# Token sums taken in place from 15 shared block buffers, weight splits in batches: attention followed by a fast maxout product

## The chip, the core and the metric

The kernel runs on one core of one Trainium2 chip. The metric is the device time in microseconds of one execution. The engines are TensorE (PE; its weight loads are PEld), VectorE (DVE), ScalarE (ACT), GpSimd (POOL) and SyncE (SP), which issues almost all DMAs from one queue, in order.

## What is computed

Sigmoid attention for 8 batches of 12 heads (448 tokens, head size 64), and then a product network on the 3584 tokens of 768 features, all in float32:

```python
scores = scale * np.matmul(q, k.transpose(0, 1, 3, 2)) - np.log(S)
attn = 1.0 / (1.0 + np.exp(-scores))
out = np.matmul(attn, v)                   # then heads are put side by side: x
h = np.maximum(np.maximum(x @ w1, x @ w2), x @ w3)
return h @ w_out
```

## The kernel before

**Attention** runs over 24 units: 8 batches, and 3 groups of four heads in each. A unit makes its scores on PE, the sigmoid on ACT, and the weighted sums on PE. Each float32 operand is split into a high and a low part (`hi`, `lo`) so that PE's products keep their precision; DVE splits the queries and keys of the next unit while PE works on this one (`qk_split`, lines 362 and 363). `finish` (lines 435 to 437) brings a half unit's result out of PSUM, by an ACT copy and a DVE addition, into a tile `m0` or `m1`, of which there is one each, and SP stores it to DRAM. The next copy into the same tile waits for that store.

**The network** has three stages (w1 and w2 with w3 go through stages 0 and 1, w_out through stage 2) of four visits, one for each pair of batches: 12 visits. A visit makes a 768 by 768 block product by 15 products of sums instead of 18 plain ones (`PRODUCTS`, one step each). A step has 18 matmuls in stages 0 and 1 and 12 in stage 2. Its operands are 15 sums of weight blocks (`W_SUMS`) and blocks `b0` to `b5` of the tokens or sums of them (`X_SUMS`, 11 of these).

- **Token sums** (`token_sums`, lines 256 to 276) are made on POOL, for each pair twice, because a half holds 448 columns: SP loads a half of the six blocks into the one tile `xin`, POOL makes 11 sums into six tiles `s`, SP stores each to `t_dram`. Layer 0 (the attention's output) has its first three pairs done during attention and the fourth at the start of stage 0. Layer 1 (h) has its four pairs done from stage 1's second visit on.
- **Loads of a step** (`x_load`) bring a block or a sum, 128x896, from DRAM into one of four tiles `qk`, five steps ahead. `x_split` makes `hi` on ACT (line 321) and `lo` (line 322) on DVE or, in the five steps where DVE has results to combine, on POOL, two steps ahead.
- **Weights** come packed and are decoded in pieces (`decode`: two ACT and four DVE instructions); three pieces make a group, for which POOL makes 15 sums of 128x128 (line 206). For stage 0 DVE splits the 15 operands one by one (`w_split`, lines 236 and 237), five at the head of a unit. Later stages' operands go through DRAM and are split by `w_resplit`.

What runs where is set by the order of the calls: each engine takes its instructions in that order. `work` hands POOL its sums, weight sums first; `later` and `tick` delay stores. `take` and `give` do not exist yet.

Of the kernel before, what the change touches and what calls it, by code (L numbers as in the profile page):

```python
# [45 lines left out]
X_SUMS = (  # L46
    ("s7", "b3", "b1"),
    ("s0", "s7", "b2"),
    ("s2", "b3", "b2"),
    ("s3", "b5", "b3"),  # L50
    ("s6", "b4", "b0"),
    ("s15", "s6", "s7"),
    ("s8", "b5", "s6"),
    ("s11", "s8", "b1"),
    ("s5", "b4", "b2"),
    ("s9", "b2", "b5"),
    ("s16", "b4", "b5"),
# [22 lines left out]
def attention_then_maxout(  # L80
# [30 lines left out]
        [dram.tile([P, NK, 2 * S], F32, name=f"x_dram{layer}{p}") for p in range(PAIRS)]  # L111
        for layer in range(2)
    ]
    t_dram = [
        [dram.tile([P, len(X_SUMS), 2, S], F32, name=f"t_dram{layer}{p}") for p in range(PAIRS)]
        for layer in range(2)
    ]
# [15 lines left out]
    qk_p = pool(ctx, "qk", 4)  # L133
    xin_p = pool(ctx, "xin", 1)
    s_p = pool(ctx, "s", 6)
# [7 lines left out]
    w_ops = [None] * len(PRODUCTS)  # L143
# [51 lines left out]
    def weight_sums(st, q, kk, wd):  # L195
# [3 lines left out]
        def one(n, name, a, op, b):  # L199
            if n == 0:  # L200
                while w_splits:
                    w_split()
                blocks["all"] = sums_p.tile([P, (len(SUMMED) + len(temps)) * P], F32, name="sums")
# [5 lines left out]
            if n == len(W_SUMS) - 1:  # L209
                if st == 0:  # L210
                    w_splits.extend((i, q, kk, blocks[w]) for i, (w, *_) in enumerate(PRODUCTS))
                else:
                    later.append((now[0], store))
# [13 lines left out]
    def w_tiles(i):  # L227
        w_ops[i] = [w_p.tile([P, 3 * 2 * P], F32R, name=f"w{part}_{i}") for part in ("hi", "lo")]

    def w_split():  # L230
        i, q, kk, src = w_splits.pop(0)
        if w_ops[i] is None:
            w_tiles(i)
        cols = slice((2 * q + kk) * P, (2 * q + kk + 1) * P)
        hi, lo = (t[:, cols] for t in w_ops[i])
        pin(nc.vector.tensor_copy(out=hi, in_=src))
        pin(nc.vector.tensor_tensor(out=lo, in0=src, in1=hi.bitcast(F32), op=sub))  # L237

    def w_load(st, i):
        w_tiles(i)  # L240
        n = UNITS[st]
        dst = w_ops[i][1].bitcast(F32)[:, : n * 2 * P]
        pin(nc.sync.dma_start(
            out=dst.rearrange("p (q k c) -> p q k c", k=2, c=P),
            in_=w_dram[st][:, :, :, SLOT[PRODUCTS[i][0]]],
        ))

    def w_resplit(st, i, engine):
        cols = slice(0, UNITS[st] * 2 * P)
        hi, lo = (t[:, cols] for t in w_ops[i])  # L250
# [5 lines left out]
    def token_sums(layer, p, when):  # L256
        index = {name: k for k, (name, *_) in enumerate(X_SUMS)}
        src = x_dram[layer][p][:].rearrange("p (j two) t -> p two j t", two=2)

        def one(kk, name, a, b, r):  # L260
            if name == X_SUMS[0][0]:
                xin = xin_p.tile([P, 2 * M * S], F32, name="xin")
                pin(nc.sync.dma_start(
                    out=xin[:].rearrange("p (j t) -> p j t", j=M), in_=src[:, kk]
                ))
                r.update((f"b{k}", xin[:, k * S : (k + 1) * S]) for k in range(2 * M))
            s = r[name] = s_p.tile([P, S], F32, name="s")
            pin(nc.gpsimd.tensor_tensor(out=s, in0=r[a], in1=r[b], op=sub))  # L268
            later.append((now[0], lambda: pin(nc.sync.dma_start(
                out=t_dram[layer][p][:, index[name], kk], in_=s  # L270
            ))))

        for kk in range(2):
            r = {}
            for name, a, b in X_SUMS:
                x_work.append((1.3, when, lambda *to: one(*to), (kk, name, a, b, r)))

    def work(budget, most):
        while budget > 0:
            if w_work:  # L280
                cost, run = w_work.pop(0)
                run()
            elif x_work and most and now[0] >= x_work[0][1]:
                cost, _, run, to = x_work.pop(0)
                run(*to)
                most -= 1
            else:
                break
            budget -= cost
# [9 lines left out]
    x_raw, x_ops, xo_p = {}, {}, [hl_p]  # L299

    def x_load(g):
        if g >= total:
            return
        (st, p), name = visits[g // STEPS], PRODUCTS[g % STEPS][1]
        layer = st // LAST
        if name[0] == "b":
            j, th = divmod(int(name[1:]), 2)
            src = x_dram[layer][p][:, 2 * j : 2 * j + 2, th * S : (th + 1) * S]
        else:
            src = t_dram[layer][p][:, [s[0] for s in X_SUMS].index(name)]  # L310
        x_raw[g] = qk_p.tile([P, 2 * S], F32, name="qk")
        pin(nc.sync.dma_start(out=x_raw[g][:].rearrange("p (k s) -> p k s", k=2), in_=src))

    def x_split(g, copy, engine=nc.vector):
        if g >= total:
            return
        raw = x_raw.pop(g)
# [3 lines left out]
        pin(copy(out=hi, in_=raw))  # L321
        pin(engine.tensor_tensor(out=lo, in0=raw, in1=hi.bitcast(F32), op=sub))  # L322
        x_ops[g] = hi, lo

    def attention(stack):
# [3 lines left out]
        m_p = pool(stack, "m", 1)  # L331
# [3 lines left out]
        def load_qk(b, k):  # L335
            t = qk_p.tile([P, 2 * S], F32, name="qk")
            if b == k == 0:
                for cols in (slice(0, S + P), slice(S + P, 2 * S)):
                    pin(nc.sync.dma_start(out=t[:, cols], in_=qk[b, k, :, cols]))
            else:  # L340
                pin(nc.sync.dma_start(out=t, in_=qk[b, k]))
# [82 lines left out]
        def load(n):  # L424
# [3 lines left out]
            elif n < len(fours) + 2:  # L428
                for g in range(2):
                    x_load(2 * (n - len(fours)) + g)  # L430

        def finish(n, g, banks):
            b, f = fours[n]
            o = m_p.tile([P, S], F32, name=f"m{g}")
            pin(nc.scalar.copy(out=o, in_=banks[0][:, :S]))
            pin(nc.vector.tensor_tensor(out=o, in0=banks[1][:, :S], in1=o, op=add))  # L436
            pin(nc.sync.dma_start(
                out=x_dram[0][b // 2][:, 2 * f + g, b % 2 * S : (b % 2 + 1) * S], in_=o
            ))
# [13 lines left out]
        terms = [[(loads[0][0],) * 2]]  # L453
        end = len(fours) - 1
        for p in range(PAIRS - 1):
            token_sums(0, p, 2 * M * (p + 1) + 2)
        for n in range(len(fours)):
            ts = loads.pop(n)
            if n != 1:
                fetch()  # L460
            if n:
                if n < end:
                    vts[n + 1] = load_v(*fours[n + 1])
                for _ in range(5):
                    if w_splits:
                        w_split()
# [10 lines left out]
            if n == 0:  # L477
                held = accumulators()
                last_scores(ts, held)
                load(n + 2)  # L480
                vts[n + 1] = load_v(*fours[n + 1])
            ahead = loads.get(n + 1)
# [13 lines left out]
            if 0 < n < end:  # L496
                decode()
            tick(1)
            work(9.0, 5)
# [10 lines left out]
            if n < end:  # L510
                lasts[n + 1] = last_scores(ahead)
                load(n + 3)
            weigh(g1, vt, 1, chunks[1], True, range(1, C))
            finish(n, 1, g1)
        while w_splits:
            w_split()
# [5 lines left out]

    xo_p.append(pool(ctx, "xo", 2, reuse_waits="tile"))
    o_p = pool(ctx, "o", 3, reuse_waits="tile")
    ps_y = pool(ctx, "ps_y", 1, space=PSUM, reuse_waits="tile")

    x_load(4)
    token_sums(0, PAIRS - 1, now[0] + 1)
    layer_start = now[0]
    for p in range(PAIRS):  # L530
        token_sums(1, p, layer_start + (PAIRS + 1 + p) * STEPS + 2)
# [4 lines left out]
    def product(n, s, q):  # L536
# [6 lines left out]
        (w_hi, w_lo), (x_hi, x_lo) = w_ops[s], x_ops[n * STEPS + s]  # L543
        terms = [(w, x, k) for k in range(2) for w, x in ((w_lo, x_hi), (w_hi, x_lo), (w_hi, x_hi))]
        for m, (w, x, k) in enumerate(terms):
            pin(nc.tensor.matmul(  # L546
                ps[:, :S], w[:, (2 * q + k) * P : (2 * q + k + 1) * P], x[:, k * S : (k + 1) * S],
# [4 lines left out]
    def evacuate(n, s, q, y):  # L552
# [36 lines left out]
        elif q == UNITS[st] - 1:  # L589
            to, o = x_dram[1][p][:, M * st + i, th * S : (th + 1) * S], first[dst]  # L590
# [10 lines left out]

# [66 lines left out]
```

## Time and profile before

| | us |
|---|---|
| median of 2 runs (1005.02 to 1011.15) | 1008.09 |
| the profiled execution, whole | 1010.78 |
| its span | 1009.0 |
| attention, up to the first matmul of the network | 337.8 |
| network, first to last matmul | 664.8 |
| after the last matmul, in the span | 6.4 |
| PE busy, share of the span | 865.7 (86%) |
| DVE, ACT, POOL busy | 723.2, 494.7, 551.5 |

The busy time of DVE and POOL holds time in which an instruction had been issued and did not yet run. `PEclk` in the rows is the clock that was granted to PE, as a share of 2.4 GHz; 0.5 is its lower level.

### The profile page before, as it was taken

How to read it: one execution, taken by the hardware profiler on the slowest of the kernel's cores; microseconds unless marked ns; L12 is line 12 of the kernel's file. 1: busy time of each engine (PE TensorE's matmuls, PEld its weight loads, DVE VectorE, ACT ScalarE, POOL GpSimd, SP SyncE). 2: the span in 40 equal slices, each digit the busy share in tenths (PEclk: the TensorE clock that was granted, in tenths of full speed). 3: DMA queues.
4: the chain of work that ended last, by engine and by line, in shares of the span. 5: the costliest groups of instructions: out<-in, count | busy, mean ns of one | idle time of the engine just before them, and what ended most of it. 6: DMA issues, size and time to landing. Idle time of an engine off the chain costs nothing.

```text
span 1009.0 us, 15279 instructions
## 1 busy us (share of the span) xinstructions
PE 865.7 (86%) x5302; PEld 701.2 (69%) x5302; DVE 723.2 (72%) x1041; ACT 494.7 (49%) x698; POOL 551.5 (55%) x499
## 2 busy tenths in 40 slices
PE   9998958767684989998999989999999782958997
PEld 5554435434352678887999979888999672847986
DVE  5588575958583786899976988898886682544654
ACT  6886646546563543544445553434434451434462
POOL 0215345244615497578614754494956966759313
PEclk9999978797887898999999989999999897988999
DMA  7666477547763987877757764868798886989884
GB/s 251 228 212 236 136 296 261 201 167 272 266 216 130 354 304 217 291 240 255 262 184 252 245 215 159 281 207 283 256 285 285 284 287 219 348 283 329 304 267 164
DMA packets 127468, 250.57 MB, mean 248 GB/s; under 512 B 11168, under 2 KB 87712, under 8 KB 127392
## 3 DMA queue, kind: packets, MB, share of 16 engines
q1 hardware_dynamic: 127248, 249.49, 73.3%
q8 instruction: 42, 0.69, 0.3%
q14 instruction: 34, 0.28, 0.1%
q10 hardware_dynamic: 144, 0.11, 0.0%
HBM read 166.33 MB, written 83.23 MB: 247 GB/s over the span
## 4 chain that ended last, share of the span: by engine, by line
PE 47%; POOL 15%; DMA 15%; DVE 13%; issue 6%; ACT 2%; SPq 1%; DVEq 0%; POOLq 0%; ACTq 0%
PE y L546 37%; POOL s L268 8%; DMA t_dram<-s 6%; POOL sums L206 5%; PE ps_s L381 4%; DVE lo L322 2%; PE ps_s L405 2%; POOL lo L322 2%; DMA qk<-t_dram 2%; PE ps_av L405 2%; DMA xin<-x_dram 2%; DMA x_dram<-m 2%; DVE wd L186 1%; DVE wd L182 1%; DVE wlo L237 1%
## 5 line engine op out<-in xcount | busy, mean ns | idle before, releaser
L546 PE MATMUL y<-lo,whi 128*128 128x448 f32 x960 | 353.6, 368 | 46.7 <-POOL lo L322 45.7
L546 PE MATMUL y<-hi,wlo 128*128 128x448 f32 x960 | 354.0, 369 | 22.3 <-DVE c L576 12.8
L546 PE MATMUL y<-hi,whi 128*128 128x448 f32 x960 | 352.9, 368 | 0.0
L321 ACT CAST hi<-qk 128x896 fp32r<-128x896 f32 x178 | 164.9, 946 | 159.0 <-PE y L546 78.7
L268 POOL TENSOR_TENSOR s<-xin 128x448 f32<-128x448 f32 x112 | 152.0, 1377 | 142.5 <-DMA xin<-x_dram 70.2
L546 PEld LDWEIGHTS y<-lo,whi 128*128 128x128 f32 x960 | 183.7, 191 | 63.4 <-POOL lo L322 48.2
L546 PEld LDWEIGHTS y<-hi,wlo 128*128 128x128 f32 x960 | 183.5, 191 | 40.7 <-issue 20.7
L322 DVE TENSOR_TENSOR lo<-qk,hi 128x896 fp32r<-128x896 f32 x121 | 159.9, 1322 | 54.7 <-ACT hi L321 54.7
L546 PEld LDWEIGHTS y<-hi,whi 128*128 128x128 f32 x960 | 183.8, 191 | 12.5
L322 POOL TENSOR_TENSOR lo<-qk,hi 128x896 fp32r<-128x896 f32 x59 | 131.5, 2254 | 77.4 <-ACT hi L321 76.8
L351 ACT ACTIVATE a<-ps_s,bias_s 128x896 f32<-128x896 f32 x121 | 116.5, 1016 | 47.8 <-PE ps_s L381 46.5
L206 POOL TENSOR_TENSOR sums<-wd,wd 128x128 f32<-128x128 f32 x128 | 80.6, 649 | 59.0 <-DVE wd L187 38.0
L381 PE MATMUL ps_s<-hi 64*128 64x448 f32 x240 | 55.1, 455 | 64.3 <-DVE m L436 47.7
L381 PEld LDWEIGHTS ps_s<-hi 64*128 64x128 f32 x240 | 26.6, 217 | 88.3 <-DVE m L436 52.1
L570 ACT COPY d<-y 128x448 f32<-128x448 f32 x64 | 34.1, 535 | 80.4 <-PE y L546 76.9
L268 POOL TENSOR_TENSOR s<-s,xin 128x448 f32<-128x448 f32 x32 | 46.4, 1451 | 32.4 <-DMA t_dram<-s 30.6
L405 PE MATMUL ps_av<-a,v 64*64 64x448 f32 x576 | 62.6, 536 | 0.0
L576 DVE TENSOR_TENSOR c<-c,y 128x448 f32<-128x448 f32 x32 | 19.2, 614 | 56.6 <-PE y L546 56.6
L405 PE MATMUL ps_s<-a,v 64*64 64x448 f32 x576 | 59.7, 545 | 0.0
L363 DVE TENSOR_TENSOR lo<-qk,hi 128x896 fp32r<-128x896 f32 (+4 forms) x51 | 57.8, 1134 | 1.8
L186 DVE CUSTOM_DVE_ANT_0 wd<-wraw,wd 128x768 uint16<-128x768 uint16 x48 | 32.2, 670 | 29.4 <-ACT wraw L177 24.9
L252 POOL TENSOR_TENSOR wlo<-wlo,whi 128x768 fp32r<-128x768 f32 (+1 forms) x20 | 38.0, 1912 | 27.7 <-ACT whi L251 27.7
(73 smaller groups left out, 1144.4 us busy)
## 6 DMA issues: line engine op xcount, KB each, us to landing
qk<-t_dram SPq DMA_DIRECT2D x132, 448.0 KB, 4.8
t_dram<-s SPq DMA_DIRECT2D x176, 224.0 KB, 6.1
xin<-x_dram SPq DMA_DIRECT2D x16, 1344.0 KB, 8.4
qk<-x_dram SPq DMA_DIRECT2D x48, 448.0 KB, 4.7
qk<-qk SPq DMA_DIRECT2D x47, 448.0 KB, 4.7
wraw<-w SPq DMA_DIRECT2D x36, 384.0 KB, 5.8
v<-v SPq DMA_DIRECT2D x24, 448.0 KB, 6.3
x_dram<-m SPq DMA_DIRECT2D x48, 224.0 KB, 4.6
```

Of the source, the lines that this page charges most:

```text
L186: pin(nc.vector.tensor_tensor(out=bits, in0=bits, in1=low, op=ALU.add))
L206: pin(nc.gpsimd.tensor_tensor(out=blocks[name], in0=blocks[a], in1=blocks[b], op=add if op == "+" else sub))
L252: pin(engine.tensor_tensor(out=lo, in0=lo.bitcast(F32), in1=hi.bitcast(F32), op=sub))
L268: pin(nc.gpsimd.tensor_tensor(out=s, in0=r[a], in1=r[b], op=sub))
L321: pin(copy(out=hi, in_=raw))
L322: pin(engine.tensor_tensor(out=lo, in0=raw, in1=hi.bitcast(F32), op=sub))
L351: pin(nc.scalar.activation(out=a, in_=banks[:, :, :S], func=AF.Sigmoid, bias=bias_s, scale=scale))
L363: pin(nc.vector.tensor_tensor(out=lo[:, cols], in0=t[:, cols], in1=high.bitcast(F32), op=ALU.subtract))
L381: pin(nc.tensor.matmul(bank[e][:, :S], kt[r, S + c * P : S + (c + 1) * P], qt[r, :S], start=n == 0, stop=n == len(terms) - 1,))
L405: pin(nc.tensor.matmul(ps[e * D : (e + 1) * D, :S], vt[rows, (g * C + c) * 2 + e], chunks[c][rows, e], start=c == 0 and not (ahead and r = ...
L546: pin(nc.tensor.matmul(ps[:, :S], w[:, (2 * q + k) * P : (2 * q + k + 1) * P], x[:, k * S : (k + 1) * S], start=new and m == 0, stop=m == ...
L570: pin(nc.scalar.copy(out=mine[dst], in_=y))
```

## The change

**Buffers.** The tiles `qk` (4), `xin`, `s` (6) and `m0`, `m1` go. In their place are 15 tiles `raw` of 128x896 that everybody takes and gives back (`take`, `give`). If none is free, `take` issues delayed stores early until one is.

**Attention's results** stay in the tile in which `finish` writes them: the two halves of a unit are the two halves of one block. The sums of a pair are made from these tiles, whole (128x896), as soon as the blocks are there (`COME`): two after the unit whose number modulo 6 is 2, four after 4, five after 5. All four pairs are done so; the last nine sums of the last pair fall into the last unit and stage 0. Sums and blocks are still stored and reloaded for stages 0 and 1.

**Layer 1** is loaded (six blocks a visit), summed by POOL (`H_SUMS`) and split from the same tiles: no store to `t_dram`, no reload. Sums of visit n are made from six steps ahead of it to its fourth step.

**Order.** `work` gives POOL token sums first. `w_split` makes its 15 pairs in four batches, two batches a unit, at least one unit after the sums. Steps are split three ahead (`SPLIT`), loaded up to eight ahead (`AHEAD`), and in stage 2 every `lo` is on DVE.

```diff
+    slots = list(range(15))
+
+    def take():
+        while not slots:
+            later.pop(0)[1]()
+        k = slots.pop(0)
+        t = raw_p.tile([P, 2 * S], F32, name=f"raw{k}")
+        return t, k
+
+    def give(raw):
+        slots.append(raw[1])
...
-    def w_split():
-        i, q, kk, src = w_splits.pop(0)
+    def w_split(lag):
+        if not w_splits or w_splits[0][0] + lag > now[0]:
+            return
+        _, part, q, kk, sums, wd = w_splits.pop(0)
...
+        rows, src = (
+            (slice(0, 6), sums[:, 0:6]),
+            (slice(n, n + 2), threes[0][:, 0::2]),
+            (slice(6, n), sums[:, 6:n]),
+            (slice(n + 2, n + 4), threes[1][:, 0:2]),
+        )[part]
...
-            s = r[name] = s_p.tile([P, S], F32, name="s")
-            pin(nc.gpsimd.tensor_tensor(out=s, in0=r[a], in1=r[b], op=sub))
...
+    def x_sum(r, name):
+        _, a, b = X_SUMS[INDEX[name]]
+        r[name] = take()
+        pin(nc.gpsimd.tensor_tensor(out=r[name][0], in0=r[a][0], in1=r[b][0], op=sub))
...
+        def store():
+            pin(nc.sync.dma_start(out=t_dram[p][:, INDEX[name]], in_=r[name][0]))
+            if not keep:
+                give(r.pop(name))
...
         def finish(n, g, banks):
             b, f = fours[n]
-            o = m_p.tile([P, S], F32, name=f"m{g}")
+            p, k = b // 2, 2 * f + b % 2
+            if g == 0:
+                blocks[p][f"b{k}"] = take()
+            block = blocks[p][f"b{k}"][0]
+            o = block[:, g * S : (g + 1) * S]
             pin(nc.scalar.copy(out=o, in_=banks[0][:, :S]))
             pin(nc.vector.tensor_tensor(out=o, in0=banks[1][:, :S], in1=o, op=add))
...
-                for _ in range(5):
-                    if w_splits:
-                        w_split()
...
+            w_split(1)
+            w_split(1)
             tick(1)
-            work(9.0, 5)
+            work(20.0, 5)
...
-            x_load(g + 5)
+            x_load(g + 1 + AHEAD)
...
-            x_split(g + 2, nc.scalar.copy, nc.gpsimd if busy else nc.vector)
+            for at in (g + 2, g + 3) if g == 0 else (g + SPLIT,):
+                x_split(at, nc.scalar.copy, nc.gpsimd if busy and st < LAST else nc.vector)
...
+    H_LOADS = {-10: ("b3", "b1"), -9: ("b2",), -8: ("b0",), -7: ("b5",), -6: ("b4",)}
```

On POOL, in attention, the sums of the first pair stand so before the change (`xin` and `s` are the loaded half and the sum tiles; lines 31 to 37 of the engine's order, unit 8 on):

```order
L268 TENSOR_TENSOR s<-xin 128x448
L268 TENSOR_TENSOR s<-s,xin 128x448
L268 TENSOR_TENSOR s<-xin 128x448 x3
L268 TENSOR_TENSOR s<-s 128x448
L268 TENSOR_TENSOR s<-xin,s 128x448
```

and so in the change (`raw_N` is one use of a shared buffer; 750, 886 and so on are attention's blocks; units 5 and 6):

```order
L277 TENSOR_TENSOR raw_859<-raw_750,raw_629 128x896
L277 TENSOR_TENSOR raw_861<-raw_859,raw_367 128x896
L277 TENSOR_TENSOR raw_863<-raw_750,raw_367 128x896
L277 TENSOR_TENSOR raw_865<-raw_593,raw_859 128x896
L277 TENSOR_TENSOR raw_993<-raw_886,raw_750 128x896
L277 TENSOR_TENSOR raw_995<-raw_367,raw_886 128x896
L277 TENSOR_TENSOR raw_997<-raw_886,raw_593 128x896
L277 TENSOR_TENSOR raw_999<-raw_488,raw_886 128x896
L277 TENSOR_TENSOR raw_1001<-raw_997,raw_629 128x896
L216 TENSOR_TENSOR sums<-wd_725,wd_846 128x128
```

The sums are twice as wide and half as many, they read what DVE's additions wrote and no loaded tile, they stand three units earlier, and the weight sums come behind them.

On SP, a unit with five sums before the change:

```order
L346 DMA v<-v 128x896
L269 DMA t_dram_70<-s 128x448 x5
L263 DMA xin<-x_dram_63 128x3x896
L437 DMA x_dram_64<-m_2132 128x448
L341 DMA qk<-qk 128x896 x2
```

and units 5 and 6 of the change:

```order
L293 DMA t_dram_70<-raw_593 128x896
L293 DMA t_dram_70<-raw_859 128x896
L369 DMA raw_900<-qk 128x896
L369 DMA raw_902<-qk 128x896
L471 DMA x_dram_62<-raw_886 128x896
L170 DMA wraw<-w 128x384
L374 DMA v<-v 128x896
L369 DMA raw_1051<-qk 128x896
```

The stores of attention's results stood behind the stores of sums that POOL had yet to make. Now two such stores remain ahead of loads (the second, of the sum s7, is issued early because no buffer is free), the load behind takes the buffer that this store empties, and the other sums of the pair are stored one or two units later.

On DVE, around one unit's end, five weight splits before the change (`whi`, `wlo` are their results) and then the next unit's query split:

```order
L436 TENSOR_TENSOR m_812<-ps_av,m_812 128x448
L236 CAST whi_820<-sums 128x128
L237 TENSOR_TENSOR wlo_821<-sums,whi_820 128x128
L236 CAST whi_824<-sums 128x128
L237 TENSOR_TENSOR wlo_825<-sums,whi_824 128x128
L236 CAST whi_828<-wd_355 128x128
```

and in the change, ahead of the two additions of `finish`:

```order
L198 SCALAR_TENSOR_TENSOR wd_846<-square,wd_846 128x384
L252 CAST whi<-sums 128x6x128
L253 TENSOR_TENSOR wlo<-sums,whi 128x6x128
L252 CAST whi<-wd_342 128x2x128
L253 TENSOR_TENSOR wlo<-wd_342,whi 128x2x128
L469 TENSOR_TENSOR raw_886<-ps_s,raw_886 128x448
```

The splits moved from the head of a unit, where they waited for POOL's fresh sums, to behind the decoding, where they read sums of the unit before.

## Rows read from the trace of the kernel before


**Rows 1.** The page, its first line.

```profile
span 1009.0 us, 15279 instructions
```

**Rows 2.** Stretches of attention: window, length, busy us of each engine, PEclk, DMA.

```profile
23.77:33.77 10.00, 10.00 (x104) 5.65 (x100) 6.55 (x10) 8.35 (x12) 0.00 (x0) 1.00 0.62 223
100.71:194.58 93.87, 70.64 (x604) 39.90 (x600) 65.83 (x125) 51.89 (x66) 40.99 (x52) 0.84 0.64 227
194.58:290.30 95.72, 69.81 (x604) 39.44 (x600) 65.06 (x122) 51.41 (x66) 41.75 (x52) 0.82 0.64 222
290.30:335.69 45.39, 32.44 (x304) 18.21 (x300) 23.51 (x38) 24.29 (x31) 18.94 (x23) 0.85 0.59 209
```

**Rows 3.** Visits of the network by windows: length, PE busy, PEld busy, PEclk, DMA.

```profile
519.57:573.57 54.00, 54.00 (x271) 50.63 (x270) 1.00 0.76 250
...
811.75:872.68 60.93, 40.25 (x181) 36.04 (x180) 0.83 0.80 267
872.68:927.52 54.84, 38.54 (x181) 34.67 (x181) 0.88 0.89 310
...
965.41:1002.65 37.24, 36.43 (x181) 33.48 (x180) 1.00 0.65 209
sum 664.81, PE 595.78 PEld 548.52; mean PE 49.65 PEld 45.71
```

**Rows 4.** Waits in attention, 100 to 340 us: total, times, longest.

```profile
POOL s L268 <- DMA t_dram<-s: 123.0, 10, 20.9
...
ACT m L435 <- DMA x_dram<-m: 44.2, 5, 15.0
...
DVE whi L236 <- POOL sums L206: 34.3, 4, 11.0
```

**Rows 5.** Waits in the network, 338 to 1009 us.

```profile
PE y L546 <- POOL lo L322: 45.7, 7, 15.2
```

**Rows 6.** DVE by time, a unit without POOL work: start, length, instruction.

```profile
28.68 0.63 DVE L362 CAST hi<-qk 128x896 fp32r<-128x896 f32 x1 [0.81 <-PE ps_s L381]
29.35 1.09 DVE L363 TENSOR_TENSOR lo<-qk,hi 128x896 fp32r<-128x896 f32 x1
...
31.16 1.09 DVE L363 TENSOR_TENSOR lo<-qk,hi 128x896 fp32r<-128x896 f32 x1
32.17 0.35 DVE L178 TENSOR_SCALAR wd<-wraw 128x384 uint32<-128x384 uint32 x1
...
35.02 0.61 DVE L436 TENSOR_TENSOR m<-ps_s,m 128x448 f32<-128x448 f32 x1
```

**Rows 7.** DVE by time, a unit with seven sums on POOL.

```profile
233.31 0.22 DVE L236 CAST whi<-sums 128x128 fp32r<-128x128 f32 x1
233.56 0.29 DVE L237 TENSOR_TENSOR wlo<-sums,whi 128x128 fp32r<-128x128 f32 x1
233.77 0.22 DVE L236 CAST whi<-sums 128x128 fp32r<-128x128 f32 x1
...
234.23 0.62 DVE L362 CAST hi<-qk 128x896 fp32r<-128x896 f32 x1
234.89 1.92 DVE L363 TENSOR_TENSOR lo<-qk,hi 128x896 fp32r<-128x896 f32 x1
...
245.83 0.61 DVE L436 TENSOR_TENSOR m<-ps_s,m 128x448 f32<-128x448 f32 x1
```

**Rows 8.** POOL by time, the same unit.

```profile
234.46 1.39 POOL L268 TENSOR_TENSOR s<-xin 128x448 f32<-128x448 f32 x1 [14.81 <-DMA t_dram<-s]
...
244.17 1.32 POOL L268 TENSOR_TENSOR s<-xin,s 128x448 f32<-128x448 f32 x1
```

**Rows 9.** POOL by time at three other places: 448 wide, 128 wide, 896 wide.

```profile
165.65 3.36 POOL L268 TENSOR_TENSOR s<-xin 128x448 f32<-128x448 f32 x3
...
172.47 1.29 POOL L206 TENSOR_TENSOR sums<-wd,wd 128x128 f32<-128x128 f32 x3
...
854.56 6.20 POOL L322 TENSOR_TENSOR lo<-qk,hi 128x896 fp32r<-128x896 f32 x3
```

More of the change, by code (lines that the diff above doesn't have):

```diff
@@ L210, in one @@
                 if st == 0:
-                    w_splits.extend((i, q, kk, blocks[w]) for i, (w, *_) in enumerate(PRODUCTS))
+                    w_splits.extend((now[0], part, q, kk, blocks["all"], wd) for part in range(4))
                 else:
@@ L248, in w_resplit @@
     def w_resplit(st, i, engine):
-        cols = slice(0, UNITS[st] * 2 * P)
-        hi, lo = (t[:, cols] for t in w_ops[i])
+        hi, lo = (t[:, w_row(st, i)] for t in (w_hi, w_lo))
         pin(nc.scalar.copy(out=hi, in_=lo.bitcast(F32)))
         pin(engine.tensor_tensor(out=lo, in0=lo.bitcast(F32), in1=hi.bitcast(F32), op=sub))
[L256 to L266, printed above, removed]
-            s = r[name] = s_p.tile([P, S], F32, name="s")
-            pin(nc.gpsimd.tensor_tensor(out=s, in0=r[a], in1=r[b], op=sub))
[L269 to L276, printed above, removed]
@@ L278, in work @@
     def work(budget, most):
         while budget > 0:
-            if w_work:
+            if x_work and most:
+                x_work.pop(0)()
+                most -= 1
+                budget -= 2.1
+            elif w_work:
                 cost, run = w_work.pop(0)
                 run()
[L283 to L286, printed above, removed]
+                budget -= cost
             else:
@@ L298, in attention_then_maxout, with x_block, x_load @@
     total = len(visits) * STEPS
[L299 to L312, printed above, removed]
+    x_raw, x_ops, xo_p, fetched = {}, {}, [hl_p], []
+    def x_block(layer, p, name):
+        raw = take()
+        src = x_dram[layer][p][:, int(name[1:])] if name[0] == "b" else t_dram[p][:, INDEX[name]]
+        pin(nc.sync.dma_start(out=raw[0], in_=src))
+        return raw
+    def x_load(upto):
+        while len(fetched) < min(upto, LAST * PAIRS * STEPS) and len(slots) > bool(x_work):
+            g = len(fetched)
+            x_raw[g] = x_block(0, visits[g // STEPS][1], PRODUCTS[g % STEPS][1])
+            fetched.append(g)
     def x_split(g, copy, engine=nc.vector):
@@ L511, in attention @@
                 lasts[n + 1] = last_scores(ahead)
+                for raw in loads[n + 1]:
+                    give(raw)
                 load(n + 3)
@@ L600, in attention_then_maxout, with h_step @@
     loaded = []
+    H_LOADS = {-10: ("b3", "b1"), -9: ("b2",), -8: ("b0",), -7: ("b5",), -6: ("b4",)}
+    H_SUMS = {
+        -6: ("s7", "s0"), -5: ("s2", "s3"), -3: ("s5", "s6"), -2: ("s15",), -1: ("s9",),
+        1: ("s8",), 2: ("s11",), 3: ("s16",),
+    }
+    SPLIT = 3
+    H_ENDS = {}
+    for name in [f"b{k}" for k in range(2 * M)] + list(INDEX):
+        reads = [s - SPLIT for s, (_, x, *_) in enumerate(PRODUCTS) if x == name]
+        reads += [s for s, made in H_SUMS.items() for x in made if name in X_SUMS[INDEX[x]][1:]]
+        H_ENDS.setdefault(max(reads), []).append(name)
+    h_raw = {}
+    def h_step(n, s, what):
+        if not LAST * PAIRS <= n < len(visits):
+            return
+        r = h_raw.setdefault(n, {})
+        if what == "load":
+            for name in H_LOADS.get(s, ()):
+                r[name] = x_block(1, visits[n][1], name)
+        elif what == "sum":
+            for name in H_SUMS.get(s, ()):
+                x_sum(r, name)
+        else:
+            for name in H_ENDS.get(s, ()):
+                give(r.pop(name))
     for n, (st, p) in enumerate(visits):
@@ L618, in attention_then_maxout @@
                 loaded.append((g, visits[n + 1][0], s))
+            for what in ("load", "sum", "end"):
+                h_step(n, s, what)
+                h_step(n + 1, s - STEPS, what)
             if s in DECODES.get(n, ()):
```

125 lines of the change are left out of this document (70 added, 55 removed).

## The prediction

> **What bounds the kernel now.** I read the page first: the span is 1009.0 us [rows 1], and PE, at 86% busy, is the engine that would set the time if nobody kept it waiting. So the question is where PE waits. I cut attention at equal points of its units (the starts of ACT's copy into `m`) and the network at the first matmul of each visit.
>
> In attention a unit without any POOL work takes 10.00 us, all of it PE, and DVE is idle for 10.00 − 6.55 = 3.45 us of it. The six units from 100.71 us take 93.87 us and the next six 95.72 [rows 2], though PE is busy only 70 us in each and its granted clock fell to 0.84 and 0.82. In these stretches POOL is busy 41 us. The waits say what comes last [rows 4]: POOL's sums wait 123.0 us for stores of earlier sums, DVE's weight splits 34.3 us for POOL, and ACT's copy into `m` 44.2 us in five pieces for the store of the old `m`, which stands on SP behind stores of sums that POOL has not made. DVE's order carries these waits into the chain of `hi`, `lo` and `finish` that PE needs.
>
> The network takes 664.81 us. Its cleanest visits take 54.00 us (18 matmuls a step) and 37.24 us (12 a step) [rows 3]; eight and four of these would be 8 × 54.00 + 4 × 37.24 = 581.0 us, so 83.8 us are lost. Of these 45.7 us are seven waits of PE for a `lo` on POOL [rows 5], all at the ninth step or next to it, where POOL has token sums ahead of the `lo`, and these wait for `xin` or for stores. Two of the four large ones fall into the first two visits of stage 2, 60.93 and 54.84 us long [rows 3].
>
> **What DVE and POOL cost each other.** This decides the sum, so I price it first. Without POOL work DVE's chain from a `hi` to the first addition of `finish` runs from 28.68 to 35.02, 6.34 us, and a `lo` takes 1.09 us [rows 6]. With POOL's seven sums beside it, first to last from 234.46 to 244.17 [rows 8], the same chain runs from 234.23 to 245.83, 11.60 us, and the `lo` takes 1.92 [rows 7]. That is 5.26 us for seven sums of 448 columns, 0.75 us each. POOL's own pace is 3.36 / 3 = 1.12 us for 448 columns and 6.20 / 3 = 2.07 for 896 [rows 9]. I price an 896 sum at 0.75 + (2.07 − 1.12) = 1.70 us of DVE's time: the added columns in full. The bounds are 0 (all of it falls into DVE's idle time or under instructions that don't collide) and 2.07 (all of it counts). I take 1.70 because the added part is busy time that alternates with DVE in these rows. A weight sum is 1.29 / 3 = 0.43 us [rows 9], counted in full on both sides.
>
> The Trainium skill, "SBUF — State Buffer", section "Who interferes with whom", says that a DVE instruction with two SBUF inputs excludes a GpSimd instruction that reads SBUF, and that the loser waits for the whole instruction. It speaks against wider sums: by it each costs 2.07 and not 1.70, which makes 0.37 × 11 sums × 3.3 pairs = 13 us more, 972 us. The `lo` of 1.92 us beside POOL agrees with it [rows 7].
>
> **Attention, part by part.**
>
> *Stores and reloads.* Reading the results in place removes `xin`'s loads and the waits for them, and the stores of sums no longer gate ACT. All three waits of [rows 4] lose their cause: the copy goes into a fresh buffer, and the weight splits read sums a unit old.
>
> *Weight splits.* A split of a 128x128 block comes every 233.77 − 233.31 = 0.46 us [rows 7], 15 × 0.46 = 6.9 us for a group. Batched, there are four pairs over 1920 columns. By the slopes between 128 and 896 columns (cast 0.22 to 0.62, `lo` 0.29 to 1.09 [rows 6, 7]) that is 4 × (0.15 + 0.16) + 1920 × (0.52 + 1.04) ns = 4.2 us. Two groups in six units save 5.4 us.
>
> *Sum over six units.* Before: 60.0 + 22 sums × 0.75 + 30 weight sums × 0.43 + 2 × 6.9 = 103.2; less all of DVE's idle time, 6 × 3.45 = 20.7, is 82.5 us. The store waits add 44.2 us over some 2.5 such stretches, 17.5 each: 100, against 94 to 96 measured, so the model is right to about 5 us, on the dear side. After: 60.0 + 11 × 1.70 + 30 × 0.43 + 2 × 4.2 = 100.0; less 20.7 is 79.3. I add 3 us, since nine of the eleven sums fall into two units that follow each other and cannot use the idle time of the others: 82.3 us.
>
> *The end of attention.* From 33.77 us, three such stretches end at 280.7. The last three units were 45.39 us [rows 2] and become 30.0 + 6 × 1.70 + 15 × 0.43 + 4.2 − 3 × 3.45 = 40.5: 321.2 us against 335.69. **Gain 14.5 us.**
>
> *What SP does.* Its two early stores a pair wait for POOL's sums, and loads stand behind them. I price this at nothing, because these loads bring the queries and keys of three units later, about 30 us, and POOL's phases of four or five sums last 4 × 2.07 to 5 × 2.07, 8 to 10 us. Without that cover each would cost up to the longest store wait of before, 15.0 us [rows 4].
>
> **The network.** The seven waits for a POOL `lo` go: the stage-0 sums are nearly finished before it starts, and in stage 2 no `lo` is on POOL. That is −45.7 us [rows 5]. In stage 1 `lo` of busy steps stays on POOL, beside sums that now wait for loads issued six steps or more ahead; I leave a gain and a loss there at nothing, since its clean visits are 54 us of PE and POOL's 11 sums need 23 us of it.
>
> New is the load of stage 2: 11 sums × 2.07 and 15 `lo` on DVE at 32.17 − 31.16 = 1.01 us [rows 6] exclude each other for 22.8 + 15.2 = 38.0 us in a visit of 37.24, and the sums lie in ten of its fifteen steps. A look-ahead of three steps (7.4 us) takes up the crowding. I add 0.8 us a visit for the excess and about 2.7 us for the uneven turns, 3.5 us in three visits: **+11 us**. Bounds: 0, and every `lo` waiting for a whole sum (below). Network: −45.7 + 10.5 = **−35 us**, 630 us.
>
> **Sum.** 1010.78 − 14.5 − 35 = 961.3 us by the profiled execution; this stands 0.27% above the median shown, so 961.3 × 1008.09 / 1010.78 = **959 us**.
>
> **The rivals.** *A, the forecast*: DVE and POOL take turns at about the prices above, 935 to 985 us.
>
> *B, POOL is hidden*: sums cost DVE next to nothing. For it: DVE idles 3.45 us a unit, and in stage 2 its additions read PSUM. Against it: the 5.26 us of the chain above. Six units are then 62 to 68 us; at 68, 3 × 14.3 = 43 us less, and 11 less in stage 2: 905. Stated as 880 to 935, about 910.
>
> *C, the turns cost their full price*: every sum costs 2.07 us in attention (+13), and in stage 2 every `lo` waits for a whole sum: 15 × (1.09 + 1.70) + 16 additions × 0.61 = 51.6 us a visit against 37.24, 14.4 × 3 = 43 us in place of 10.5. That is 959 + 13 + 32.5 = 1004 us, no measurable change. For it: the `lo` of 1.92; against it: three steps of look-ahead, and POOL has pauses.
>
> *D, slower*: SP's one queue is what stops. A forced store waits for POOL's sum, the loads behind it wait too, then the next unit's queries are late, DVE and POOL with them. Seven such places (two a pair); at 15.0 us each, 105 us: 1064. It decides for slower from 68 / 7 = 9.7 us each (959 + 68 = 1027). Against it stands the lead of 30 us. For it stands that 15 buffers are few when a pair holds six blocks and up to nine sums.
>
> **How the numbers follow.** A 0.52, B 0.22, C 0.19, D 0.07. The measurement tells about 2% from no change: 988 to 1028 us. A and B are faster, 0.74; C is the same, 0.19; D is slower, 0.07. The range from 905 to 1004 us leaves out D, and the outer parts of B and C, about 2 in 10 together. The forecast's own range is 935 to 985.
>
> **What would show it.** In the changed profile: no wait of POOL's token sums for a store; no wait of PE for a POOL `lo` in the first visit and in stage 2; six units in 80 to 86 us, the dear ones with four and five sums about 16 us; visits of stage 2 with sums beside them 38 to 44 us. `lo` of 2 us and more on DVE in these. Units of 10 to 11 us throughout would speak for B; visits of 50 us in stage 2 for C; PE or DVE waiting for loads of `qk` in attention, with SP waiting for POOL, for D. I am wrong as well if attention's waits do not go but move to the buffers: a copy of `finish` that waits for a buffer's last store.

## The result, and the profile after

| | before | after |
|---|---|---|
| median, us | 1008.09 | 962.59 (961.51 to 963.67) |
| span of the profiled execution | 1009.0 | 961.9 |
| first matmul of the network | 337.8 | 319.4 |
| network, first to last matmul | 664.8 | 636.2 |

After to before: 0.955, 95% interval 0.942 to 0.968. Forecast were 959 us, between 905 and 1004. (Runs below without an interval are one execution each; executions of one kernel lie within some 0.6% of their median here.) One of the four executions of the run of 888.43 us below took 939.51 us at a lower granted clock, 0.845; its ratio leaves that execution out.

The stretches of attention after, cut at the starts of ACT's copy of a unit's first half (line 468), with the columns of [rows 2]: first the two units in which the four and then the five sums of the first pair run, then two stretches of six units, then the last three.

```profile
64.90:84.90 20.00, 13.81 (x116) 8.09 (x112) 17.48 (x15) 9.08 (x13) 13.63 (x7) 0.83 0.49 172
84.90:101.80 16.90, 11.19 (x96) 6.81 (x92) 13.88 (x18) 8.81 (x12) 11.67 (x16) 0.80 0.59 196
111.90:196.10 84.20, 68.64 (x604) 39.16 (x600) 66.00 (x76) 51.88 (x67) 44.46 (x41) 0.86 0.62 220
196.10:278.70 82.60, 66.43 (x604) 38.05 (x600) 66.46 (x76) 51.49 (x67) 44.91 (x41) 0.90 0.64 223
278.70:313.70 35.00, 31.97 (x304) 18.07 (x300) 28.46 (x35) 24.94 (x32) 19.57 (x20) 0.95 0.70 265
```

Six units take 84.20 and 82.60 us where they took 93.87 and 95.72 [rows 2]. The gain is not even: of six units that follow each other, one takes 20.0 us, one 16.9 to 17.7, one 14.4 to 15.8, and three 10.1 to 10.5.

The waits in attention after (34 to 330 us; those of before are [rows 4]):

```profile
POOL raw L277 <- DVE raw L469: 121.1, 12, 37.5
...
PE ps_s L409 <- DVE raw L469: 47.5, 13, 6.9
...
ACT raw L468 <- POOL raw L277: 7.5, 3, 2.8
```

POOL now waits for DVE's additions, its operands, and for no store; ACT waits for no store, and only 7.5 us for a buffer. What PE waits for is line 469, the additions of `finish`. They come late on DVE.

The network by visits, columns as in [rows 3]: the first visit, the last of stage 1, and the four of stage 2.

```profile
319.39:384.71 65.32, 58.32 (x270) 53.65 (x271) 0.92 0.70 246
723.00:777.00 54.00, 54.00 (x271) 50.61 (x270) 1.00 0.61 201
777.00:829.77 52.77, 41.69 (x181) 35.66 (x180) 0.90 0.31 105
829.77:876.22 46.45, 39.27 (x180) 34.44 (x181) 0.96 0.36 119
876.22:918.31 42.09, 37.80 (x180) 33.22 (x181) 1.00 0.38 132
918.31:955.56 37.25, 36.53 (x180) 33.57 (x180) 1.00 0.17 62
```

The last visit of stage 1 fell from 63.04 us to 54.00, all of it PE. Stage 2 kept an excess: 52.77 and 46.45 us where it had 60.93 and 54.84 [rows 3], and the third visit grew, from 37.89 to 42.09. The two visits of before that [rows 3] leaves out:

```profile
748.71:811.75 63.04, 55.94 (x271) 51.81 (x271) 0.95 0.86 292
927.52:965.41 37.89, 36.24 (x181) 33.66 (x181) 1.00 0.89 306
```

PE's largest waits in the network after (338 to 962 us; [rows 5] is the row of before):

```profile
PE y L577 <- DVE c L607: 16.3, 11, 3.8
PE y L577 <- POOL lo L349: 4.9, 1, 4.9
```

Six of seven waits for POOL's `lo` are gone, 4.9 us of 45.7 are left. The one that is left ends at 784.66 us, at step 1 of stage 2's first visit.

### The profile page after: what moved, and what is told of

Same layout as the page of the kernel before. It is cut to its first block, busy times and chain, and to the rows that moved or that the text cites. A ratio compares the mean times of both kernels' runs of the same rounds, so it can differ in the third digit from the quotient of the medians.

```text
span 961.9 us, 14566 instructions
## 1 busy us (share of the span) xinstructions
PE 864.9 (90%) x5302; PEld 700.1 (73%) x5302; DVE 772.6 (80%) x928; ACT 499.1 (52%) x698; POOL 509.7 (53%) x392
## 4 chain that ended last, share of the span: by engine, by line
PE 59%; DVE 25%; issue 9%; POOL 2%; DMA 2%; ACT 2%; SPq 0%; DVEq 0%; ACTq 0%; POOLq 0%
PE y L577 44%; PE ps_s L409 7%; DVE lo L349 6%; DVE hi L390 4%; PE ps_s L433 3%; PE ps_av L433 2%; DVE lo L391 2%; DVE wd L197 1%; DVE wlo L253 1%; DVE d L607 1%; DVE wd L193 1%; PE ps_av L409 1%; DVE whi L252 1%; ACT a L379 1%; DVE raw L469 1%
## 5 line engine op out<-in xcount | busy, mean ns | idle before, releaser
L277 POOL TENSOR_TENSOR raw<-raw,raw 128x896 f32<-128x896 f32 x88 | 219.3, 2510 | 159.1 <-DVE raw L469 121.1
L348 ACT CAST hi<-raw 128x896 fp32r<-128x896 f32 x178 | 167.7, 943 | 225.3 <-PE y L577 168.3
L349 DVE TENSOR_TENSOR lo<-raw,hi 128x896 fp32r<-128x896 f32 x140 | 212.9, 1526 | 50.0 <-ACT hi L348 49.9
L216 POOL TENSOR_TENSOR sums<-wd,wd 128x128 f32<-128x128 f32 x128 | 89.4, 718 | 75.5 <-DVE wlo L253 33.8
L349 POOL TENSOR_TENSOR lo<-raw,hi 128x896 fp32r<-128x896 f32 x40 | 92.0, 2306 | 69.1 <-ACT hi L348 65.9
L390 DVE CAST hi<-raw 128x896 fp32r<-128x896 f32 (+4 forms) x51 | 58.1, 1140 | 39.7 <-PE ps_s L409 34.7
L391 DVE TENSOR_TENSOR lo<-raw,hi 128x896 fp32r<-128x896 f32 (+4 forms) x51 | 83.1, 1630 | 1.8
L197 DVE CUSTOM_DVE_ANT_0 wd<-wraw,wd 128x768 uint16<-128x768 uint16 x48 | 30.1, 626 | 38.5 <-ACT wraw L188 34.9
L409 PE MATMUL ps_s<-lo,hi 64*128 64x448 f32 x240 | 49.5, 409 | 0.0
```

What stands on the lines that cost most here:

```text
L197: pin(nc.vector.tensor_tensor(out=bits, in0=bits, in1=low, op=ALU.add))
L216: pin(nc.gpsimd.tensor_tensor(out=blocks[name], in0=blocks[a], in1=blocks[b], op=add if op == "+" else sub))
L277: pin(nc.gpsimd.tensor_tensor(out=r[name][0], in0=r[a][0], in1=r[b][0], op=sub))
L348: pin(copy(out=hi, in_=raw[0]))
L349: pin(engine.tensor_tensor(out=lo, in0=raw[0], in1=hi.bitcast(F32), op=sub))
L390: pin(nc.vector.tensor_copy(out=high, in_=t[:, cols]))
```

## The experiments

### The price of layer 0's sums

```diff
-        x_sum(r, name)
+        r[name] = take()
+        pin(nc.sync.dma_start(out=r[name][0], in_=qk[0, 0]))
```

> The changed kernel, but the 44 token sums of layer 0 are not made: each buffer is filled by a load of the first query-and-key block instead, so POOL has only the weight sums in attention; stores, buffers and reloads stay. Theory (turns of DVE and POOL): the sums cost what the long units show, so the units of 14 to 20 us fall to 10 to 13 (the weight splits ahead of finish remain), the first matmul of the network comes at 255 to 270 us in place of 319.4, and the first visit loses its stop of 6.7 us at step 2: whole 890 to 910. Rival (the buffers, stores and SP's order hold attention, not POOL's columns): units of 17 us and more stay, whole above 940.

Measured: 898.19 us; the first matmul of the network at 259.45 us. Two stretches of six units:

```profile
63.48:127.69 64.21, 60.97 (x604) 34.10 (x600) 50.16 (x76) 50.93 (x67) 19.78 (x30) 1.00 0.98 365
127.69:194.05 66.36, 62.71 (x604) 34.80 (x600) 50.25 (x76) 50.94 (x67) 19.80 (x30) 0.97 0.95 357
```

With the same buffers and stores, and even more loads, units take 10 to 12 us but for one of 13.9. So the sums themselves hold attention: 319.39 − 259.45 = 59.9 us. Of the 44 sums 39 begin before that first matmul in the change, so one costs 1.54 us. (The 1.36 that an expectation below uses divides by all 44.) The first visit lost only 2.6 us (62.73 us), not the 6.7 of its stop.

### The price of layer 1's sums

```diff
-                x_sum(r, name)
+                r[name] = x_block(1, visits[n][1], "b0")
```

> The changed kernel, but the 44 token sums of layer 1 are not made: each buffer is filled by a load of block b0, so POOL makes no token sum beside stage 2. Theory (every lo on DVE waits for a whole sum): the visits of stage 2, now 52.8, 46.5, 42.1 and 37.3 us, fall to 43, 39, 38 and 37: whole about 940. Rival (what DVE has to do in stage 2 by itself, 15 lo and the results, holds these visits): they keep at least half of their excess, whole above 950.

Measured: 934.05 us. Stage 2:

```profile
777.17:814.75 37.58, 36.56 (x181) 33.59 (x180) 1.00 0.84 305
814.75:851.75 37.00, 36.28 (x181) 33.66 (x180) 1.00 0.80 285
851.75:888.75 37.00, 36.28 (x181) 33.67 (x180) 1.00 0.81 287
888.75:925.91 37.16, 36.44 (x181) 33.48 (x179) 1.00 0.27 89
```

The whole excess of stage 2, 178.6 − 148.7 = 29.8 us, is the sums' on POOL: more than the theory had said, since even the first visit, with weights to split again, falls to 37.58. What that price is made of shows in the changed kernel, DVE and POOL by time in a steady stretch of stage 2:

```profile
856.96 1.14 DVE L607 TENSOR_TENSOR d<-d,y 128x448 f32<-128x448 f32 x2
858.02 2.15 DVE L349 TENSOR_TENSOR lo<-raw,hi 128x896 fp32r<-128x896 f32 x1
860.10 1.14 DVE L607 TENSOR_TENSOR u<-u,y 128x448 f32<-128x448 f32 x2
861.16 2.16 DVE L349 TENSOR_TENSOR lo<-raw,hi 128x896 fp32r<-128x896 f32 x1
```

```profile
857.11 2.11 POOL L277 TENSOR_TENSOR raw<-raw,raw 128x896 f32<-128x896 f32 x1 [1.03 <-DVE lo L349]
860.25 2.12 POOL L277 TENSOR_TENSOR raw<-raw,raw 128x896 f32<-128x896 f32 x1 [1.03 <-DVE lo L349]
```

A turn is one sum (2.11 us) and then one `lo` (1.03 us, for which POOL waits): 3.14 us. The two additions of results, which read PSUM, run beside the sum at their usual 1.14. A step of PE takes 37.24 / 15 = 2.48 us, so in such a stretch a sum costs 0.66 us: it is too long for the 1.1 us that DVE leaves free between two `lo`. The visits do not all go by this price. About 39 of the 44 sums run in stage 2, 26 us by it, but its four visits exceed 37.24 us by 15.5, 9.2, 4.9 and 0. In the first, splits of weights (`wlo`) on DVE and POOL take turns with the sums and the `lo`s too; how the 29.8 us divide between these is not shown.

### Sums in halves

```diff
-        pin(nc.gpsimd.tensor_tensor(out=r[name][0], in0=r[a][0], in1=r[b][0], op=sub))
+        for c in (slice(0, S), slice(S, 2 * S)):
+            pin(nc.gpsimd.tensor_tensor(
+                out=r[name][0][:, c], in0=r[a][0][:, c], in1=r[b][0][:, c], op=sub
+            ))
```

> The changed kernel with every token sum as two POOL instructions of 448 columns in place of one of 896. Theory (DVE and POOL take turns, one instruction each): twice as many turns, half as long; four sums meet the four split instructions and then the four decoding ones, so the long units keep their length within 1.5 us: whole 955 to 968. Rival (only the width that one instruction meets counts, and what is left of POOL's work goes into DVE's idle time): the four split instructions wait for four halves only, the units of 17 and 20 us lose 3 to 4 us each: whole 935 to 950.

Measured: 929.39 us, 33 less than with whole sums, by one edit that adds 88 instructions. Both the theory's range and the rival's lie above it. The theory was right where turns are packed: the unit of 20.0 us takes 20.1. It failed where DVE leaves gaps. The unit after it fell from 16.9 to 14.7, the first matmul of the network came at 302.55, 16.8 us earlier, and stage 2 is nearly clean but for its first visit:

```profile
759.70:808.04 48.34, 39.36 (x182) 34.49 (x180) 0.93 0.33 115
808.04:845.91 37.87, 36.28 (x181) 33.67 (x180) 1.00 0.42 152
845.91:883.10 37.19, 36.34 (x182) 33.59 (x180) 1.00 0.39 143
```

DVE by time in this kernel, in the same kind of stretch, with POOL at half sums throughout:

```profile
841.85 1.15 DVE L610 TENSOR_TENSOR t<-t,y 128x448 f32<-128x448 f32 x2
842.91 1.08 DVE L352 TENSOR_TENSOR lo<-raw,hi 128x896 fp32r<-128x896 f32 x1
843.91 1.15 DVE L610 TENSOR_TENSOR d<-y,d 128x448 f32<-128x448 f32 x2
```

```profile
833.70 16.50 POOL L278 TENSOR_TENSOR raw<-raw,raw 128x448 f32<-128x448 f32 x9
```

A `lo` takes 1.08 us and no longer 2.15: a half sum, 1.12 us by [rows 9], is done while DVE adds from PSUM. The last visit takes 38.18 us, so 161.6 − 148.7 = 12.9 us of stage 2's excess of 29.8 are left, 10.8 of them in the first visit.

### Before with more buffers

```diff
-    s_p = pool(ctx, "s", 6)
+    s_p = pool(ctx, "s", 11)
-        m_p = pool(stack, "m", 1)
+        m_p = pool(stack, "m", 2)
```

(and the size that makes room, `dynamic_dma_scratch_size=2048`, as in the change)

> The kernel before, with more buffers and nothing else: 11 tiles s in place of 6, two tiles for each m in place of one. Theory (attention's gain came from taking store waits out of POOL's and ACT's queues): the 44.2 us of ACT's waits for the store of m go, POOL's 123 us of waits for stores shrink by more than half, and the first matmul of the network comes at 316 to 325 us in place of 337.8: whole 980 to 993. Rival (the sums themselves hold attention through DVE, the stores only fill the time): first matmul at 331 or later, whole above 998.

Measured: 983.63 us, first matmul of the network at 310.98 us. So attention alone gains 26.9 us from buffers, more than the whole change gains there (18.5) and more than the expectation allowed (the first matmul at 316 to 325). What the tiles `s` and what the tiles `m` give, and whether the size that makes room does anything by itself, no run separates. The wait of ACT for the store of `m`, 44.2 us [rows 4], is gone; POOL's for stores, 123.0 us, went from first to small:

```profile
POOL s L268 <- DMA xin<-x_dram: 56.4, 6, 12.6
...
POOL s L268 <- DMA t_dram<-s: 8.0, 5, 2.8
```

The network stayed: 664.5 us.

### Before with every `lo` on DVE

```diff
-            x_split(g + 2, nc.scalar.copy, nc.gpsimd if busy else nc.vector)
+            x_split(g + 2, nc.scalar.copy, nc.vector)
```

> The kernel before, with one thing changed: every lo of a step is made on DVE, none on POOL. Theory (the network's gain comes from taking PE's operand out of POOL's queue): the seven waits of 45.7 us go, the network takes 620 to 635 us in place of 664.8 and attention stays at 338, whole 965 to 980. Rival (DVE then has too much in the steps with results, so that POOL was needed): network above 650, whole above 995.

Measured: 994.54 us, network 652.9: 12 us less there. The theory missed by 14.5 us and more. The rival's number is met in the network (above 650) and missed by half a microsecond in the whole, but its cause, too much work on DVE, is not what holds PE here. What held PE in place of POOL's `lo` shows with both edits on the kernel before:

> The kernel before with both earlier edits: more buffers (11 s, two of each m) and every lo on DVE. Theory (in the network the round trip of layer 1's sums, loaded half, sum, store, reload, hi, is what stays late once POOL makes no lo): stops of about 10 us in the first two visits of stage 2 remain, at steps 11 and 12, network 648 to 656, attention to 311: whole 968 to 976. Rival (with more buffers the sums come in time): network 635 or less, whole below 960, which would leave the in-place sums of layer 1 without a gain.

Measured: 967.97 us; first matmul at 310.6, network 649.3. The stops moved from step 9 to steps 11 and 12 of the first two visits of stage 2. The waits around one of them (810 to 825 us):

```profile
ACT hi L321 <- DMA qk<-t_dram: 14.5, 2, 12.1
DVE lo L322 <- ACT hi L321: 10.5, 2, 10.4
...
PE y L546 <- DVE c L576: 10.1, 1, 10.1
```

PE is held by results on DVE, these by a `lo`, this by `hi` on ACT, and this by a reload. The sum that is reloaded had long been made: POOL was done with that pair's sums at 699.42 us. But the reload stands on SP behind a load of `xin` for a later pair, and this waits for POOL to be done with the one `xin` (SP's waits, 795 to 825 us):

```profile
SPq L263 <- POOL s L268: 7.3, 1, 7.3
```

The load of `xin` goes out at 808.65, the reload at 810.41, and it lands at 818.01. So the wait for POOL's `lo`, 15.2 us, was covering a second one of 10: the reload's place in SP's order. The expectation had the times and the steps. Of its cause, a sum's whole way through DRAM, only the last part was late: the reload, and not the sum. Whether a second tile `xin` would have removed this stop no run shows.

These two edits bring the kernel before within 5.4 us of the change, about the spread of single executions. Against them the change's attention is 8.8 us longer (319.39 and 310.59) and its network 13.1 us shorter (636.2 and 649.3).

### Weight splits: later, or one by one

```diff
-            w_split(1)
-            w_split(1)
             tick(1)
...
             finish(n, 1, g1)
+            w_split(1)
+            w_split(1)
...
```

> The changed kernel with one thing moved: the two batches of weight splits stand on DVE behind the two additions of a unit's finish and no longer ahead of them. Theory (a unit is long because finish, which frees PE's PSUM bank, comes late on DVE, and PE pays a stop with a lower clock on top): the three units of 14.4 to 15.8 us with two sums fall to 10.5 to 12, those of 17 and 20 lose 2 to 3 us each: 20 to 30 us less, whole 932 to 943. Rival (DVE's work per unit decides, wherever it stands: the splits then delay the next unit's query split): within 8 us of 962.

Measured: 954.79 us, 0.947 of before (0.943 to 0.952): 8 us less than the change, not 20 to 30; the rival's number is met. The three units of 14.4 to 15.8 us still take 14. The splits, put behind `finish`, meet the sums there. DVE in this kernel, where the two sums of a unit begin at 115.17:

```profile
115.86 2.13 DVE L253 TENSOR_TENSOR wlo<-sums,whi 128x640 fp32r<-128x640 f32 x1
117.91 2.18 DVE L252 CAST whi<-wd 128x256 fp32r<-128x256 f32 x1
```

A split of 0.28 us takes 2.18. A narrow instruction of DVE waits as long for a sum as a wide one.

The other edit of the splits makes each batch out of single blocks at the same place:

> The changed kernel with the weight splits of a batch made one block of 128 columns at a time (15 pairs a group as before the change), at the same places. Theory (the batches stand ahead of finish, so what they save comes off the unit's end): 6.9 us a group in place of 4.2 by rows of before, 1.35 us more in each of the units with two batches, with PE's lower clock up to 2: 15 units of that kind give 15 to 30 us more, whole 975 to 990. Rival (the saving was hidden in DVE's idle time): within 6 us of 962.

Measured: 983.15 us, 20.6 more, and the first matmul of the network at 336.26 us, 16.9 later. The batches' saving is real and lies on the path: the stops in front of a unit's scores are 7.8, 7.0 and 3.8 us long where they were 6.2, 5.7 and 2.6.

### Part of stage 2 undone

```diff
-nc.gpsimd if busy and st < LAST else nc.vector
+nc.gpsimd if busy else nc.vector
```

> The changed kernel with one part undone: in stage 2 the lo of the five steps with results stands on POOL again. Theory (with the sums made six steps ahead POOL is seldom late, but a lo of 2.1 us behind a sum of 2.1 to 2.5 us takes its turn with DVE as well): the visits of stage 2 get 2 to 8 us longer each, whole 970 to 990. Rival (the sums being early was all that counted, and POOL relieves DVE): no change or a gain, whole 950 to 965.

Measured: 971.59 us, 9 more in one run. Stage 2's visits take 49.1, 46.2, 45.3 and 45.1 us in place of 52.8, 46.5, 42.1 and 37.3: 7.1 us more in all. The whole is in the theory's range, the visits are not: the first is 3.7 us shorter, the second as long, and only the last two are longer, by 3.2 and 7.8 us, with a stop of 5 us for POOL's `lo` at step 1 of each.

### Sums on DVE

```diff
-        pin(nc.gpsimd.tensor_tensor(out=r[name][0], in0=r[a][0], in1=r[b][0], op=sub))
+        pin(nc.vector.tensor_tensor(out=r[name][0], in0=r[a][0], in1=r[b][0], op=sub))
```

> The changed kernel with all 88 token sums on DVE in place of POOL, in the same order, so that in attention they stand ahead of finish. Theory (a sum on POOL costs DVE more than making it itself: 1.36 us by the run without layer 0's sums, 60 us for 44, against 1.09 for such an instruction on DVE; in stage 2, 29.6 us for 44 sums against 0.67): attention gains 10 to 20 us, stage 2 gains or loses up to 10; whole 935 to 960. Rival (DVE is the busiest engine after PE, and 88 more instructions of 1.09 us, 96 us, make it the bound): whole above 970.

Measured: 937.17 us, 0.929 of before (0.923 to 0.934). 88 more instructions on the second busiest engine make the kernel 25 us faster: the first matmul of the network comes at 309.85, 9.5 us earlier, and the network takes 621.4 us, 14.7 less (stage 2 alone 15.4 less, more than the theory's 10). Then, in attention, the sums behind `finish`, two a unit:

```diff
-            work(20.0, 5)
+            work(20.0, 0)
 ...
             finish(n, 1, g1)
+            for _ in range(2):
+                if x_work:
+                    x_work.pop(0)()
```

> As the run with all token sums on DVE, but in attention the sums stand behind a unit's two additions, at most two a unit, where DVE waits 2.2 us for PE. Theory (what costs is a late finish, not DVE's total): two sums of 1.09 us fit there, units with sums take 10 to 13 us, the first matmul of the network comes at 265 to 285 us, whole 895 to 930. Rival (DVE's total decides): as the other run within 8 us.

Measured: 888.43 us, 0.881 of before (0.876 to 0.886), the first matmul of the network at 258.53, no unit above 11.1 us: better than the theory's range, and far from the rival's. Last, the same in attention, with layer 1's sums on POOL in halves:

> Layer 0's sums on DVE behind finish, at most two a unit (as in the run of that kind); layer 1's sums on POOL in halves of 448 columns. Theory (a half sum fits between DVE's lo instructions, under two additions that read PSUM, where a whole one does not): the visits of stage 2 are 48, 38, 37 and 38 us and the visit ahead of them 54 in place of 58, so 4 to 9 us less than 888: whole 879 to 885. Rival (in either place the work of the sums is what counts): 887 to 892.

Measured: 883.13 us, 0.878 of before (0.876 to 0.880), the fastest version. The visits of stage 2 take 47.47, 38.07, 38.01 and 38.17 us and the one ahead of them 54.00, close to the expected. Six units, and DVE behind the additions of one:

```profile
63.36:127.73 64.37, 61.56 (x604) 33.48 (x600) 61.41 (x88) 51.38 (x68) 22.10 (x30) 1.00 0.82 275
```

```profile
67.76 0.61 DVE L476 TENSOR_TENSOR raw<-ps_av,raw 128x448 f32<-128x448 f32 x1
68.29 2.08 DVE L282 TENSOR_TENSOR raw<-raw,raw 128x896 f32<-128x896 f32 x2
70.29 0.62 DVE L397 CAST hi<-raw 128x896 fp32r<-128x896 f32 x1
```

DVE is busy 61.41 of 64.37 us and PE stays at full clock: the two sums, 2.08 us, stand where DVE had waited for PE's scores.

## Why the prediction was right

The time, the direction and the two places of the gain held. Several of the terms inside did not have the size that I gave them, and they cancelled in part: that the total came within 0.4% is in good part luck.

| step | forecast | measured |
|---|---|---|
| six units of attention | 82.3 | 84.2 and 82.6 |
| its last three units | 40.5 | 35.0 |
| start of its last copy | 321.2 | 313.7 |
| network | 630 | 636.2 |
| cost of sums in stage 2 | 10.5 | 29.8 |

**Attention: the waits.** All three of [rows 4] went, as said, and the buffers are the cause: with more of them the kernel before gains 26.9 us there. That the sums are taken in place was not needed for it. The start of the last copy came 22.0 us earlier and not 14.5, but the first matmul of the network only 18.5, since four sums of the last pair run in the last unit and hold up DVE's addition at 318.72, for which PE waits 3.4 us before that matmul.

**Attention: DVE and POOL.** I gave an 896 sum 1.70 us of DVE's time. Beside POOL the four splits of a unit's queries and keys take from 77.42 to 88.14:

```profile
77.42 2.56 DVE L390 CAST hi<-raw 128x896 fp32r<-128x896 f32 x1 [2.17 <-PE ps_s L409]
80.02 2.87 DVE L391 TENSOR_TENSOR lo<-raw,hi 128x896 fp32r<-128x896 f32 x1
82.81 2.51 DVE L390 CAST hi<-raw 128x896 fp32r<-128x896 f32 x1
85.36 2.86 DVE L391 TENSOR_TENSOR lo<-raw,hi 128x896 fp32r<-128x896 f32 x1
88.14 0.34 DVE L189 TENSOR_SCALAR wd<-wraw 128x384 uint32<-128x384 uint32 x1
```

These 10.72 us are 3.49 without sums, from 28.68 to 32.17 [rows 6]: 1.81 us for each of the four sums that meet them. The step was right to 7%. The Trainium skill, "SBUF — State Buffer", section "Who interferes with whom", has the loser blocked for the whole instruction, 2.07 us here: the four come to about nine tenths of it, and in the turns of stage 2 above each engine waits until the other's instruction has ended.

What I had wrong is where it counts. I subtracted DVE's idle time from a sum over six units, as if it could be moved. The dear units were to take 16 us and take 20.00 and 16.90. The weight sums do not fill the short units either: those from 127.54 us on lie in the unit of 15.8 us. That the total over six units came out is two errors that nearly cancel. Without sums the run above takes 64.21 and 66.36 us, where my terms leave 82.3 − 18.7 − 3 = 60.6: the rest was dearer than I gave. The same units of the change take 83.4 us (64.88 to 148.30) and 83.0 (to 231.33), so eleven sums cost 19.2 and 16.7 us, where I gave 21.7 with the crowding.

**Weight splits.** 5.4 us over six units was the forecast, some 22 for 24; undoing the batches costs 20.6, of which 16.9 lie before the network.

**The network.** −45.7 us for the `lo` was nearly right as a count of waits. The 4.9 us that are left are at a place that I had ruled out: the first `lo` of stage 2 are split three steps ahead, in stage 1, where busy steps still use POOL. As a gain the term was right for stages 0 and 1 in sum: 45.7 − 29.2 = 16.5 us of stops, 473.9 − 457.6 = 16.3 us gained. In stage 2 the stops were 29.2 us, and its time fell only by 190.9 − 178.6 = 12.3. The term for the turns, +10.5, is the mis-sized one: it was 29.8. I had let a look-ahead of three steps take up the crowding and put the sums into ten of fifteen steps; the code puts eleven into eight, each turn adds 0.66 us, eleven of them nearly use up the 7.4 us of the look-ahead, and in the first visit the weights' splits come on top. On the other side 12.9 us of waits that I had left in place went as well, since without its sums stage 2 is clean. So 19.3 us too few and 12.9 too many left an error of 6.4, which is luck.

The run with every `lo` on DVE shows that the removal of POOL's `lo` alone is worth 12 us in the network: behind it stood reloads that wait on SP behind a load of `xin`. In stage 2 the change has neither. I had found the right wait and missed the second under it.

**The rivals.** B is out as a whole, though its grain of truth is the halves: what fits under DVE's additions from PSUM is hidden. C named the mechanism of stage 2 and put it at 43 us; it came to 29.8, and its sign, a visit of 50 us, showed in the first visit alone (52.77). D's place exists and does no harm: in attention SP's loads wait for POOL six times, 6.8 us at most,

```profile
SPq L369 <- POOL raw L277: 26.3, 6, 6.8
```

and no DVE instruction there waits for such a load. The point from which it decides was 9.7 us.

**What I did not foresee.** The first visit keeps 65.32 of its 66.78 us. Its stop at step 9 went and a new one came at step 2, 6.7 us of PE waiting for DVE's additions: four sums of the last pair run there, and the decoding that stands ahead of the additions takes a turn with each. One wait of POOL's sums for a store is left as well, where I had said none: 9.4 us before the sum at 341.87, with no stop of PE above 1.5 us behind it in that visit.

```profile
325.88 2.28 DVE L189 TENSOR_SCALAR wd<-wraw 128x384 uint32<-128x384 uint32 x1
328.19 2.32 DVE L193 SCALAR_TENSOR_TENSOR wd<-wraw,wd 128x384 uint32<-128x384 uint32 x1
```

## What to carry to other kernels

When two engines exclude each other, cost an instruction by the longest gap that the other leaves, not by its share of busy time: 896 columns on POOL cost 1.54 us in attention and 0.66 in a steady stretch of stage 2, two times 448 less (33 us over all 88 sums), and on DVE itself 1.09 in a place where DVE waits. And before a removed wait is booked as a gain, ask what would hold the same instruction without it: here, a reload that was late by two thirds as much, because of its place in a queue.

## What was not expected of the hardware

- A stop costs PE more than its length. In a unit of 15.8 us, where others take 10.1, PE stops for 2.64 us, and its matmuls behind it are longer:

```profile
125.85 0.37 PE L409 MATMUL ps_s<-hi,lo 64*128 64x448 f32 x2
128.86 0.74 PE L409 MATMUL ps_s<-hi 64*128 64x448 f32 x2 [2.64 <-DVE raw L469]
129.40 0.57 PE L409 MATMUL ps_s<-lo,hi 64*128 64x448 f32 x2
```

  This is the lower granted clock, 0.50 from 128.80 to 134.80 us, and the unit with its stop of 2.6 us is 5.7 us longer than the others. Two more units with a stop of 2.6 to 2.7 us take 14.56 and 14.45 us, 4.4 longer, at 0.72 and 0.73 in the 6.2 us behind the stop. In the unit of 11.02 us that starts at 43.71 PE stops for 0.87 us, and its clock stays at 1.00.
- POOL takes about twice DVE's time for such a sum, 2.07 against 1.09 us, and the exclusion turns most of that into DVE's own time. The Trainium skill, "GPSIMD Engine Reference", section "3.1 Elementwise — side-by-side cycle accounting", gives 1.96 for the ratio with 2048 elements; here it is 1.90.
- DVE's additions that read PSUM keep their 0.61 us beside any POOL work: in the changed kernel all of them, in the network and in `finish`, take 0.60 to 0.63 us.
